# Attention, soft mixture of experts and a feed-forward layer in one kernel: the AV products of a pair of heads in one run, on nineteen exp tiles

## The chip, the cores and the metric

The kernel runs on one core of a Trainium2 chip. Its time is the device time of one execution in microseconds (us). The kernel before took 464.92 us, the median of three runs (464.62 to 466.56). One further execution was profiled.

## What is computed

Sixteen heads (2 batches of 8) of 768 tokens with 64 features. Each query and key is hashed by the signs of six projections, and a query attends only to keys of its own bucket. The output of attention is the input of a soft mixture of experts, and that of a feed-forward layer with g = h - tanh(h).

```python
q_bits = (np.einsum('bhsd,dk->bhsk', q, proj) > 0).astype(np.int64)
k_bits = (np.einsum('bhsd,dk->bhsk', k, proj) > 0).astype(np.int64)
mask = q_bucket[:, :, :, None] == k_bucket[:, :, None, :]
scores = np.where(mask, scale * np.matmul(q, k.transpose(0, 1, 3, 2)), -1000000000.0)
attn = np.exp(scores - np.max(scores, axis=-1, keepdims=True))
attn = attn / (np.sum(attn, axis=-1, keepdims=True) + 1e-09)
out = np.matmul(attn, v)
...
d = softmax of x @ phi over the tokens; slot_out[e] = np.maximum(slot_input[e] @ w1[e], 0.0) @ w2[e]
g = h - np.tanh(h)      # h = x @ w_in
return (g @ w_out).astype(np.float32)
```

## The kernel before, in words

Heads are worked on in eight pairs, 0 to 7. For each pair:

- xq and xk arrive by DMA. ScalarE (and GpSimd for pair 0) writes their high parts into the operands QA and KA (`his`, L378). The low parts go into QB and KB: by way of a PSUM tile `hp` that ScalarE writes (`hi_ps`, L407) and VectorE subtracts (`lo_ps`, L416), or on GpSimd for pair 0.
- The hash bits are four products with `projb` on 32 columns of the array (`pb`, L333; L355 for pairs 0 and 1), a comparison on VectorE, and rows of plus or minus a large number, placed below the features in QA and KA.
- The row maxima: 18 PSUM tiles `pm` (L444), each reduced by VectorE (L446). `m_fin` turns them with one product `pc` (L454), makes a row on VectorE (`zrow`, `row`, L457 and L458) and sends it by DMA into QA.
- The scores: 18 PSUM tiles `pst` (nine for each head; two products each, with QA and KA and then QB and KB, L503), each followed by an exponential on ScalarE into a tile `e` (L505) of the pool `e_p`, which has 12 tiles. GpSimd adds the tiles `e` up (L515).
- The AV products: nine units `a`. Each takes a tile of head 0 and one of head 1 against v (`tv`), both heads at once on 64 columns of the array (L532), into two PSUM tiles `pav`. A first product of `pav`, with `zrw` and `vzw` on all 128 columns (L526), opens each.
- Then come sums over `e` (`pr`, L546, on 32 columns), transposes (`prt`, `px`), and logits (`pl`).

Beside this, VectorE and ScalarE convert w_in from 64-bit numbers, in 16 pieces. One conversion is a ScalarE pass (`cg`, L179) and three VectorE passes (`cl`, `cl`, `win`, L183, L192, L197).

PSUM tiles of this stage come from six banks in turn. Every engine works through its instructions in the order in which the program issues them. That order is written out by hand: START is a list of units for the first stage, STEP a list for each of pairs 0 to 6, LAST that for pair 7. In them `m` is a tile of maxima, `s0` and `s1` one of scores of head 0 and 1, `a` an AV unit, `wl` and `wc` the loading and conversion of a piece of w_in, `g0` to `g2` and `l0` to `l2` the high and low parts, `lp` the loading of a piece of weights. A unit of which everything is done is skipped.

The weights of the experts arrive in pieces of 1 MB, in slots that are opened in groups (RING) as memory of the attention stage is given up. After attention comes the mixture of experts (from about 250 us), and from about 315 us the feed-forward loop.

Of the kernel before, what the change touches and what calls it, by code (L numbers as in the profile page):

```python
# [132 lines left out]
def body(ctx: ExitStack, tc: tile.TileContext, q, k, v, proj, phi, w1, w2, w_in, w_out, cst, out, dbg=None):  # L133
# [114 lines left out]
    def attention():  # L248
# [80 lines left out]
        def bits(i):  # L329
            pb = psum("pb")  # L330
            for g in range(4):
                x = (xqs, xks)[g // 2][i]
                nc.tensor.matmul(pb[32 * g:32 * g + 32, :HALF], projb, x[:, (g % 2) * HALF:(g % 2 + 1) * HALF],  # L333
                                 start=True, stop=True, tile_position=(0, 32 * g))
# [14 lines left out]
        def bits0(i, which):  # L349
            x = (xqs, xks)[which][i]  # L350
            w = (512, S - 512)
            bt0[which] = [e_p.tile([P, 512], F32, tag="e", name="bt0")[64:64 + 4 * NB, :n] for n in w]
            pbs = [psum("pb") for _ in w]
            for j, (c0, c1) in enumerate(((0, 512), (512, S))):
                nc.tensor.matmul(pbs[j][64:96, :w[j]], projb, x[:, c0:c1], start=True, stop=True, tile_position=(0, 64))  # L355
            for j in range(2):
                nc.vector.tensor_scalar(bt0[which][j], pbs[j][64:64 + 4 * NB, :w[j]], 0.0, None, ALU.is_gt)

        def rows0(i, which, h, eng):
            rs = slice(64, 64 + 4 * NB)  # L360
            X, o = ((QA, C_FIRST), (KA, C_FIRST + 2 + 2 * h))[which]
            w = ct[rs, o:o + 2]
            for (c0, c1), b, e in zip(((0, 512), (512, S)), bt0[which], "av" if eng == "s" else 2 * eng):
                y = X[i][h][rs, c0:c1]
                if e == "a":
# [328 lines left out]
        def unit(w, i):  # L694
            if w in ("m", "s0", "s1", "a", "ap", "wl", "wc", "lp", "warm", "keep", "const", "e"):
                if w == "m" and nm.get(i) == 2 * len(SEQ) - 1:
                    return
            elif (w, i) in done:
                return
            else:  # L700
                done.update({(w, i), (w.replace("hv", "h").replace("hp", "h").replace("lv", "l"), i)})
# [12 lines left out]
            elif w[:2] in ("bq", "bk"):  # L714
                bits0(i, "qk".index(w[1]))
            elif w[:2] in ("wq", "wk"):
                rows0(i, "qk".index(w[1]), int(w[2]), w[3])
# [682 lines left out]
```

## Time and profile before

| | |
|---|---|
| median of three runs | 464.92 us |
| the profiled execution | 464.5 us, its span 462.7 us |
| TensorE (PE) | 442.7 us busy, 96% of the span |
| VectorE (DVE) | 330.5 us, 71% |
| ScalarE (ACT) | 271.8 us, 59% |
| GpSimd (POOL) | 289.3 us, 63% |
| mean granted clock of TensorE | 0.99 |

A share of the whole span is a mean over three stages with different limits. Through the attention stage VectorE is busy for nine tenths and more, behind it less. TensorE counts as busy whenever one of its overlapping matmuls is under way, so that its share says little. What a matmul costs is the distance from its start to the start of the next one. Idle time stands in brackets with what ended it.

### The profile page before, as it was taken

The page shows a single profiled execution, that of the slowest core. Times are in us where ns is not written, and L with a number is a line of the kernel's source. Part 1 is how long each engine was busy: PE and PEld are TensorE (multiplying, and loading weights), DVE is VectorE, ACT ScalarE, POOL GpSimd, SP SyncE. Part 2 cuts the span into 40 slices and gives each one's busy share as a digit, 9 for nine tenths or more (in the row PEclk, how much of TensorE's full clock was granted, in tenths as well). Part 3 has the DMA queues.
Part 4 walks back from the last instruction along what each step waited for, and adds up shares of the span by engine and source line. Part 5 has one row for each costly group of instructions (what it writes and reads, how often), then busy time and mean ns, then how long its engine had stood idle before and what let it go on. Part 6 is the DMA issues. An engine that isn't in the chain of part 4 may idle for free. (4 is left out here: it accounts for less than half of the span.)

```text
span 462.7 us, 7587 instructions
## 1 busy us (share of the span) xinstructions
PE 442.7 (96%) x2639; PEld 296.6 (64%) x2639; DVE 330.5 (71%) x592; ACT 271.8 (59%) x521; POOL 289.3 (63%) x291
## 2 busy tenths in 40 slices
PE   7589999999999999999999999999999999999995
PEld 3455565656666575766765544567777778888883
DVE  3999798897989969577173438579998976544441
ACT  4526676756776565654450111278889887666661
POOL 4976977889697896958871110025888884444450
PEclk9889999999999999999999999999999999999998
DMA  6337337153633509449539999992000003000004
GB/s 195 110 98 221 125 98 219 41 170 127 189 125 106 167 15 298 178 142 326 216 157 379 421 416 417 419 419 83 2 1 2 0 0 137 1 1 1 0 1 144
DMA packets 18342, 71.32 MB, mean 154 GB/s; under 512 B 3668, under 2 KB 4792, under 8 KB 13176
## 3 DMA queue, kind: packets, MB, share of 16 engines
q1 hardware_dynamic: 17976, 70.75, 43.5%
q8 instruction: 23, 0.38, 0.4%
q14 instruction: 23, 0.19, 0.1%
q10 hardware_dynamic: 320, 0.01, 0.0%
HBM read 60.08 MB, written 3.15 MB: 137 GB/s over the span
## 5 line engine op out<-in xcount | busy, mean ns | idle before, releaser
L505 ACT ACTIVATE e<-pst 128x512 f32<-128x512 f32 x144 | 79.9, 598 | 44.6 <-PE pst L503 40.9
L515 POOL TENSOR_TENSOR es<-es,e 128x512 f32<-128x512 f32 x73 | 92.9, 1288 | 13.1 <-ACT e L505 13.0
L446 DVE TENSOR_REDUCE mx<-pm 128x1 f32<-128x512 f32 x144 | 90.2, 682 | 10.7 <-PE pm L444 9.8
L532 PE MATMUL pav<-e,tv 128*64 128x512 f32 (+1 forms) x384 | 70.5, 496 | 0.0
L503 PE MATMUL pst<-QA,KA 128*128 128x256 f32 (+1 forms) x192 | 67.7, 367 | 0.8 <-DVE mx L446 0.4
L503 PE MATMUL pst<-QB,KB 128*128 128x256 f32 (+1 forms) x192 | 62.2, 338 | 0.0
L1221 DVE SCALAR_TENSOR_TENSOR ph<-win,ph 128x512 f32<-128x512 f32 (+1 forms) x64 | 35.7, 558 | 32.2 <-ACT win L1216 30.8
L444 PE MATMUL pm<-KA,QA 96*128 96x512 f32 x192 | 51.5, 369 | 2.8 <-DVE QA L368 2.4
L1252 POOL TENSOR_TENSOR split<-win,split 128x512 fp32r<-128x512 f32 x31 | 44.8, 1447 | 14.2 <-ACT split L1247 14.2
L1273 PE MATMUL po<-w,split 128*128 128x512 f32 x128 | 51.0, 399 | 0.0
L1271 PE MATMUL po<-w,split 128*128 128x512 f32 x128 | 50.6, 396 | 0.0
L515 POOL TENSOR_TENSOR es<-e 128x512 f32<-128x512 f32 x30 | 39.2, 1316 | 18.1 <-PE pr L546 18.0
L1272 PE MATMUL po<-w,split 128*128 128x512 f32 x128 | 50.5, 394 | 0.0
L444 PEld LDWEIGHTS pm<-KA,QA 96*128 96x128 f32 x192 | 34.0, 197 | 24.1 <-ACT e L505 7.3
L503 PEld LDWEIGHTS pst<-QA,KA 128*128 128x128 f32 x192 | 36.1, 188 | 20.2 <-DVE mx L446 7.1
L1252 POOL TENSOR_TENSOR ghl<-win,ghl 128x256 fp32r<-128x256 f32 x32 | 24.2, 757 | 37.0 <-ACT ghl L1247 37.0
L1216 ACT ACTIVATE win<-ph 128x512 f32<-128x512 f32 (+1 forms) x64 | 30.8, 481 | 23.0 <-PE ph L1209 22.3
L1222 DVE SCALAR_TENSOR_TENSOR win<-win,ph 128x512 f32<-128x512 f32 (+1 forms) x64 | 35.5, 555 | 8.7 <-DVE ph L1221 0.5
L532 PEld LDWEIGHTS pav<-e,tv 128*64 128x64 f32 x384 | 24.1, 136 | 27.1 <-issue 20.4
L1217 ACT ACTIVATE win<-win,ct 128x512 f32<-128x512 f32 (+1 forms) x64 | 39.5, 617 | 2.1
L503 PEld LDWEIGHTS pst<-QB,KB 128*128 128x128 f32 x192 | 36.4, 189 | 2.0
L1273 PEld LDWEIGHTS po<-w,split 128*128 128x128 f32 x128 | 24.0, 188 | 7.7 <-POOL split L1252 2.7
(236 smaller groups left out, 818.4 us busy)
## 6 DMA issues: line engine op xcount, KB each, us to landing
w<-in_moe_w_dram SPq DMA_DIRECT2D x32, 1024.0 KB
raw<-in_moe_w_in_dram SPq DMA_DIRECT2D x16, 512.0 KB
w<-in_moe_w_out_dram SPq DMA_DIRECT2D x8, 1024.0 KB
xq<-in_q_dram SPq DMA_DIRECT2D x8, 384.0 KB
xk<-in_k_dram SPq DMA_DIRECT2D x8, 384.0 KB
tv<-in_v_dram SPq DMA_DIRECT2D x8, 384.0 KB
out_dram<-win SPq DMA_DIRECT2D x12, 256.0 KB
QB<-QA SPq DMA_DIRECT2D x10, 192.0 KB
```

The costliest lines, as they stand in the source:

```text
L444: nc.tensor.matmul(pm[:, j * 256:j * 256 + c1 - c0], QA[s][h][:96, c * P:(c + 1) * P], KA[s][h][:96, c0:c1], start=True, stop=True)
L446: nc.vector.reduce_max(m, pm.rearrange("p (c k) -> p c k", c=len(cs)), axis=AX.X)
L503: nc.tensor.matmul(pst[:, j * 256:j * 256 + c1 - c0], K[h][:, c * P:(c + 1) * P], Q[h][:, c0:c1], start=x == 0, stop=x == 1)
L505: nc.scalar.activation(e, pst, AF.Exp, scale=0.125)
L515: eng.tensor_tensor(q[0], y, e, ALU.add)
L532: nc.tensor.matmul(pav[i][k][64 * h:64 * h + 64, :], tv[i][:, h, c, :], e2[h][:, j * 256:j * 256 + c1 - c0], start=False, stop=c == KT - 1 ...
L1217: nc.scalar.activation(w, z, AF.Square, bias=ct[:, C_QA:C_QA + 1])
L1221: nc.vector.scalar_tensor_tensor(self.ph[p], z, Q_C, self.ph[p], ALU.mult, ALU.mult)
L1252: (eng or nc.gpsimd).tensor_tensor(gl[p], g, gh[p].bitcast(F32), ALU.subtract)
L1271: nc.tensor.matmul(po, gh[p][:, us], wo.half(f, 0), start=f == 0, stop=False)
L1272: nc.tensor.matmul(po, gh[p][:, us], wo.half(f, 1), start=False, stop=False)
L1273: nc.tensor.matmul(po, gl[p][:, us], wo.half(f, 0), start=False, stop=f == NF - 1)
```

## The change

- Nineteen tiles `e` in place of twelve for pairs 0 to 5: seven come from a new pool `ex_p`, which is given up in pair 6. Eighteen tiles hold all the exponentials of a pair.
- New lists of units. FIRST is for pair 0, STEP for pairs 1 to 5, STEP2 for pair 6; START is rewritten, LAST is as it was. In STEP the nine AV units of the pair before stand at the head, then the scores and the maxima.
- `fy` and `vy` are `fz` and `v2` (the rows for `zrw`, `vzw`) of the same pair in place of the next.
- For pairs 0 and 1 the bits are one PSUM tile of four products on 32 columns, compared in place (VectorE reads and writes PSUM), and the rows are written from there. Before it was two tiles for each of q and k, compared into four tiles of `e_p`.
- `projb` arrives laid out by the host, in one DMA in place of a memset and four.
- One slot for weights less is opened after pair 5 and one more in pair 6.

```diff
+WIDE, NE1, NE2 = 5, 12, 7
-RING, HOLD = (4, 2, 2, 4, 3, 2, 3, 1), 4
+RING, HOLD = (4, 1, 3, 4, 3, 2, 3, 1), 4
-STEP = ("a a a m xe s0 g1 m a m l1 s1 s0 s1 m s0 m m g0 l0 m xr s1 h1 m m s0 m a m m wl m g2 s1 lp l2 s0 v wl a d m wc "
+STEP = ("a a a a a a a a wc a d g0 l0 fy h1 g1 wc l1 g2 h0 h3 lp l2 vy m m wl s0 m lp s0 s1 v xe m m qk m s0 m e xr b m "
...
     def consts2(phiB, projb, blk):
-        nc.vector.memset(projb, 0.0)
-        for h in range(2):
-            for j in range(2):
-                c0 = 2 * NB * h + NB * j
-                nc.scalar.dma_start(out=projb[64 * h:64 * h + 64, c0:c0 + NB], in_=proj)
+        nc.scalar.dma_start(out=projb, in_=proj)
...
-        e_p = pool("e_p", 12)
+        e_p = pool("e_p", NE1)
...
+        ex_p = pool("ex_p", NE2, wide_x)
...
-        def bits0(i, which):
-            x = (xqs, xks)[which][i]
-            w = (512, S - 512)
-            bt0[which] = [e_p.tile([P, 512], F32, tag="e", name="bt0")[64:64 + 4 * NB, :n] for n in w]
-            pbs = [psum("pb") for _ in w]
-            for j, (c0, c1) in enumerate(((0, 512), (512, S))):
-                nc.tensor.matmul(pbs[j][64:96, :w[j]], projb, x[:, c0:c1], start=True, stop=True, tile_position=(0, 64))
+        def halves(i, pb):
+            for g in range(4):
+                x = (xqs, xks)[g // 2][i]
+                nc.tensor.matmul(pb[32 * g:32 * g + 32, :HALF], projb, x[:, (g % 2) * HALF:(g % 2 + 1) * HALF],
+                                 start=True, stop=True, tile_position=(0, 32 * g))
+
+        def bits0(i):
+            pb = bt0[i] = psum("pb")
+            halves(i, pb)
+            nc.vector.tensor_scalar(pb[:, :HALF], pb[:, :HALF], 0.0, None, ALU.is_gt)
+
+        def rows0(i, which, h, eng):
+            X, o = ((QA, C_FIRST), (KA, C_FIRST + 2 + 2 * h))[which]
             for j in range(2):
...
+                rs = slice(32 * (2 * which + j), 32 * (2 * which + j) + 4 * NB)
+                y, b, w = X[i][h][64:64 + 4 * NB, j * HALF:(j + 1) * HALF], bt0[i][rs, :HALF], ct[rs, o:o + 2]
...
-            e = e_p.tile([P, 512], F32, tag="e", name="e")
+            turn[0] += i <= WIDE
+            e = (ex_p if i <= WIDE and turn[0] % (NE1 + NE2) >= NE1 else e_p).tile([P, 512], F32, tag="e", name="e")
...
-            for u in STEP if i < NPR - 1 else LAST:
+            for u in FIRST if i == 0 else STEP if i <= WIDE else STEP2 if i < last else LAST:
...
-                if i == 6 and len(slots) == sum(RING[:2]) and not xqs and not xks:
+                if i == 6 and len(slots) == sum(RING[:2]) and not xqs and not xks and (not queue or queue[0][0] > WIDE):
                     xq_x.close()
+                    wide_x.close()
                     open_ring(RING[2], rctx)
```

The tables move instructions. The first place is TensorE around the AV products of a pair in the middle of the stage. `pav` are the AV products, and `pst` and `pm` scores and maxima. Before, one of a pair's visits to the 64 columns follows the other after eight matmuls on 128:

```order
L526 MATMUL pav<-zrw,vzw 128x512
L532 MATMUL pav<-e,tv 64x512 x2
L444 MATMUL pm<-KA_135,QA_131 128x512
L444 MATMUL pm<-KA_135,QA_131 128x256 x2
L444 MATMUL pm<-KA_135,QA_131 128x512
L503 MATMUL pst<-QA_130,KA_134 128x512
L503 MATMUL pst<-QB_138,KB_141 128x512
L503 MATMUL pst<-QA_129,KA_133 128x512
L503 MATMUL pst<-QB_137,KB_140 128x512
L532 MATMUL pav<-e,tv 64x512 x2
L444 MATMUL pm<-KA_135,QA_131 128x512
```

In the changed kernel, the same products of one pair:

```order
L457 MATMUL pc<-ct,mh 12x128
L532 MATMUL pav<-zrw,vzw 128x512
L538 MATMUL pav<-e,tv 64x512 x4
L532 MATMUL pav<-zrw,vzw 128x256
L538 MATMUL pav<-e,tv 64x256 x4
L538 MATMUL pav<-e,tv 64x512 x4
L538 MATMUL pav<-e,tv 64x256 x4
L538 MATMUL pav<-e,tv 64x512 x4
L538 MATMUL pav<-e,tv 64x256 x4
L490 MATMUL pv<-va,ones_62 128x128
L447 MATMUL pm<-KA_135,QA_131 128x512 x2
```

All nine units stand between `pc` and the next pair's maxima, with only the second `zrw` product among them. Before, a pair's AV products stand in five such runs (2, 2, 6, 2 and 12 matmuls).

The second place is TensorE at the bits (`pb`) and the sums (`pr`), both on 32 columns. Before, the bits follow the fourth AV run and stand apart from the sums:

```order
L532 MATMUL pav<-e,tv 64x512 x2
L454 MATMUL pc<-ct,mh 12x128
L333 MATMUL pb<-xq,projb 32x384 x2
L333 MATMUL pb<-xk,projb 32x384 x2
L503 MATMUL pst<-QA_129,KA_133 128x256
L503 MATMUL pst<-QB_137,KB_140 128x256
L503 MATMUL pst<-QA_129,KA_133 128x256
L503 MATMUL pst<-QB_137,KB_140 128x256
```

In the changed kernel:

```order
L447 MATMUL pm<-KA_135,QA_131 128x512
L552 MATMUL pr<-es_706,ones_62 32x384
L552 MATMUL pr<-es_807,ones_62 32x384
L552 MATMUL pr<-es_706,ones_62 32x128
L552 MATMUL pr<-es_807,ones_62 32x128
L552 MATMUL pr<-es_873,ones_62 32x256
L552 MATMUL pr<-es_909,ones_62 32x256
L355 MATMUL pb<-xq,projb 32x384 x2
L355 MATMUL pb<-xk,projb 32x384 x2
L447 MATMUL pm<-KA_135,QA_131 128x512
```

The bits now stand right behind the sums. With the AV products, a pair now goes three times to fewer than 128 columns, where it went seven times.

The third place is VectorE at the end of a pair's maxima. Before, the conversion of a piece of w_in comes behind the bits and the reciprocals, while maxima and low parts are spread over the pair:

```order
L451 TENSOR_REDUCE mh<-mx 128x12
L457 TENSOR_SCALAR zrow<-pc 12x128
L458 SCALAR_TENSOR_TENSOR row<-zrow,pc 12x128
L336 TENSOR_SCALAR bt<-pb 128x384
L570 TENSOR_SCALAR rs<-prt 128x6x2
L573 RECIPROCAL rs<-rs 128x12
L183 TENSOR_SCALAR cl<-raw 128x512
L192 SCALAR_TENSOR_TENSOR cl<-cg,cl 128x512
L197 SCALAR_TENSOR_TENSOR win<-raw,cl 128x512
```

In the changed kernel:

```order
L449 TENSOR_REDUCE mx<-pm 128x2
L454 TENSOR_REDUCE mh<-mx 128x12
L460 TENSOR_SCALAR zrow<-pc 12x128
L461 SCALAR_TENSOR_TENSOR row<-zrow,pc 12x128
L188 TENSOR_SCALAR cl<-raw 128x512
L197 SCALAR_TENSOR_TENSOR cl<-cg,cl 128x512
L202 SCALAR_TENSOR_TENSOR win<-raw,cl 128x512
L419 TENSOR_TENSOR KB_143<-xk,hp 64x512
L419 TENSOR_TENSOR KB_144<-xk,hp 64x512
L188 TENSOR_SCALAR cl<-raw 128x512
L197 SCALAR_TENSOR_TENSOR cl<-cg,cl 128x512
L202 SCALAR_TENSOR_TENSOR win<-raw,cl 128x512
```

Two conversions and the eight low parts (`KB`, `QB`; two are seen here) now stand together behind `mh` and `pc`, which is to say beside TensorE's AV run.

The fourth place is VectorE at the program's start. Before:

```order
L301 MEMSET QA_128 64x1536
L357 TENSOR_SCALAR bt_168<-pb 24x512
L357 TENSOR_SCALAR bt_169<-pb 24x256
L357 TENSOR_SCALAR bt_176<-pb 24x512
L357 TENSOR_SCALAR bt_177<-pb 24x256
L368 TENSOR_SCALAR QA_128<-bt_176,ct 24x512
L368 TENSOR_SCALAR QA_128<-bt_177,ct 24x256
L446 TENSOR_REDUCE mx<-pm 128x1 x2
```

In the changed kernel:

```order
L307 MEMSET QA_131 64x1536
L174 MEMSET ones_62 128x32
L361 TENSOR_SCALAR pb<-pb 128x384
L371 TENSOR_SCALAR QA_131<-pb,ct 24x384 x2
L449 TENSOR_REDUCE mx<-pm 128x1 x2
L449 TENSOR_REDUCE mx<-pm 128x2
L449 TENSOR_REDUCE mx<-pm 128x1 x2
```

One comparison in PSUM stands for four, and the rows of QA come in equal halves.

## Rows read from the trace of the kernel before

**Rows 1.** The page's first line, the profiled span
```profile
span 462.7 us, 7587 instructions
```

**Rows 2.** Stretches: length, busy us (count) of engines, clock, DMA share, GB/s
```profile
94.60:122.10 27.50, 27.50 (x167) 17.16 (x166) 24.73 (x46) 18.53 (x35) 22.93 (x24) 1.00 0.45 135
242.00:290.00 48.00, 46.98 (x424) 24.10 (x424) 24.06 (x45) 5.96 (x12) 4.85 (x17) 1.00 0.98 401
```

**Rows 3.** Waits of PE, 60 to 245 us: total, times, longest
```profile
PE pm L444 <- DVE cl L192: 0.2, 1, 0.2
```

**Rows 4.** PE in order of time: start us, length us, line, tiles, count
```profile
111.25 3.66 PE L532 MATMUL pav<-e,tv 128*64 128x256 f32 x24
...
138.82 3.66 PE L532 MATMUL pav<-e,tv 128*64 128x256 f32 x24
142.41 0.50 PE L444 MATMUL pm<-KA,QA 96*128 96x512 f32 x1
...
142.99 0.40 PE L503 MATMUL pst<-QB,KB 128*128 128x512 f32 x1
143.22 0.63 PE L444 MATMUL pm<-KA,QA 96*128 96x512 f32 x3
143.69 0.40 PE L503 MATMUL pst<-QA,KA 128*128 128x512 f32 x1
...
152.48 0.40 PE L503 MATMUL pst<-QB,KB 128*128 128x512 f32 x1
152.80 1.08 PE L532 MATMUL pav<-e,tv 128*64 128x512 f32 x4
153.81 0.73 PE L444 MATMUL pm<-KA,QA 96*128 96x512 f32 x3
154.38 0.28 PE L503 MATMUL pst<-QA,KA 128*128 128x256 f32 x1
```

**Rows 5.** Waits of DVE over two pairs: first and last of six
```profile
DVE mx L446 <- PE pm L444: 1.1, 2, 0.6
...
DVE bt L336 <- PE pb L333: 0.4, 2, 0.2
```

**Rows 6.** DVE in order of time, one pair from 94.6 us
```profile
94.47 4.28 DVE L446 TENSOR_REDUCE mx<-pm 128x1 f32<-128x512 f32 x7
98.78 0.85 DVE L416 TENSOR_TENSOR KB<-xk,hp 64x256 fp32r<-64x256 f32 x2
...
101.24 0.69 DVE L183 TENSOR_SCALAR cl<-raw 128x512 uint32<-128x512 uint32 x1
...
103.38 2.47 DVE L446 TENSOR_REDUCE mx<-pm 128x2 f32<-128x512 f32 x4
...
106.69 0.28 DVE L457 TENSOR_SCALAR zrow<-pc 12x128 fp32r<-12x128 f32 x1 [0.56 <-PE pc L454]
...
117.29 1.37 DVE L416 TENSOR_TENSOR QB<-xq,hp 64x512 fp32r<-64x512 f32 x2
```

**Rows 7.** ACT in order of time, one conversion
```profile
109.18 0.67 ACT L179 ACTIVATE cg<-raw 128x512 f32<-128x512 f32 x1
```

**Rows 8.** The first stage in order of time, all engines
```profile
1.20 2.48 ACTq L167 DMA_DIRECT2D projb<-in_proj_dram  x4
...
1.58 0.43 SPq L320 DMA_DIRECT2D xk<-in_k_dram  x1
...
5.37 0.84 ACT L378 ACTIVATE KA<-xk 64x768 fp32r<-64x768 f32 x1 [0.37 <-DMA xk<-in_k_dram]
...
11.27 2.36 DVE L368 TENSOR_SCALAR QA<-bt,ct 24x512 fp32r<-24x512 f32 x2
...
13.96 5.47 DVE L446 TENSOR_REDUCE mx<-pm 128x1 f32<-128x512 f32 x9 [0.33 <-PE pm L444]
...
54.42 0.56 DVE L336 TENSOR_SCALAR bt<-pb 128x384 f32<-128x384 f32 x1 [0.22 <-PE pb L333]
...
60.27 1.36 DVE L446 TENSOR_REDUCE mx<-pm 128x1 f32<-128x512 f32 x2
```

More of the change, by code (lines that the diff above doesn't have):

```diff
@@ L61 @@
 FORD = [4 * q + 2 * h + i for h in range(2) for q in range(4) for i in range(2)]
-RING, HOLD = (4, 2, 2, 4, 3, 2, 3, 1), 4
-START = ("warm.4 const.1 qk.0 const.0 hp2.0 keep.1 oi.0 const.2 h0.0 bk.0 bq.0 keep.3 wq0v.0 kc.0 wl.0 keep.3 wk0a.0 "
[3 rows of a table removed]
-        "keep.1 oi.2 wl.0").split()
-STEP = ("a a a m xe s0 g1 m a m l1 s1 s0 s1 m s0 m m g0 l0 m xr s1 h1 m m s0 m a m m wl m g2 s1 lp l2 s0 v wl a d m wc "
-        "lp v1 e m s0 s0 a wl a lp a e s1 lp m m h0 s1 s0 qk m v2 h3 s1 e lp a f2 lp b s0 x2 e fz wc s1 wc s1 lg lp h2 "
-        "x3 a a wl lp").split()
+RING, HOLD = (4, 1, 3, 4, 3, 2, 3, 1), 4
+START = ("oi.0 qk.0 h1.0 const.1 const.0 warm.4 const.2 keep.1 hp3.0 keep.3 h0.0 wl.0 b0.0 wk0a.0 hp2.0 kc.0 wq0v.0 wl.0 "
+        "m.0 keep.1 m.0 m.0 qk.1 l1.0 m.0 wk1a.0 m.0 m.0 m.0 m.0 keep.1 m.0 v.0 wq1a.0 m.0 keep.3 m.0 m.0 keep.3 m.0 "
+        "v1.0 d.0 h2.1 h3.1 l0.0 m.0 fa.0 m.0 m.0 m.0 h1.1 v.1 oi.1 keep.1 b0.1 m.0 l3.0 fb.0 h0.1 wc.0 wq0a.1 wl.0 "
+        "kc.1 s0.0 keep.1 l2.0 oi.2 wl.0 qk.2 fz.0 wk1a.1 s0.0 wk0v.1 s0.0 wc.0 a.0 wq1a.1 s0.0 v2.0 wc.0 s0.0 s0.0").split()
+FIRST = ("wc wc lp lp a a a a a a a g0 g1 h1 fy wl m vy g2 l0 a a l1 l2 s0 h0 s0 s1 m m s1 s1 v m wl m h3 qk m m d m m "
+        "xe s1 h2 b m m s0 m e wl lg m s1 m s1 m s0 lp e s0 wl xr v1 lp m x3 x2 m s1 s0 s1 e m s1 lp lp s0 s0 f2 s0 s0 "
+        "wc s1 e").split()
+STEP = ("a a a a a a a a wc a d g0 l0 fy h1 g1 wc l1 g2 h0 h3 lp l2 vy m m wl s0 m lp s0 s1 v xe m m qk m s0 m e xr b m "
+        "h2 x2 m m v1 wl s0 lp m s1 lp s0 m m lg x3 s1 m m s1 m s0 m wc e s0 s0 s1 s1 s1 m wl s0 s1 s0 lp lp e s1 f2 e "
+        "s1 wl").split()
+STEP2 = ("m m a a a a a a vy s0 a a a a fy g1 l1 m s0 s0 m a m s1 h1 m s0 s1 m m m s1 g0 wl m xe d l0 xr m m v s0 v1 a a "
+        "e s1 g2 m l2 a a m lp m e e lp lp s0 wl s1 wl lp b x2 qk wc s1 m m s0 v2 e lp m s1 wc h2 a a a f2 wc h3 lp h0 "
+        "fz lp s0 wl s0 s1 x3 s1 lg lp").split()
 LAST = ("a a s0 a lp xe a a a s0 lp lp a a lp s0 s0 lp s0 s1 s1 s0 s1 xr s0 s1 s1 lp s1 s1 lp a a lp a s0 x2 s1 s0 lg "
@@ L120, in constants @@
                     o = C_FIRST + 2 * (g // 2 + g // 2 * h)
-                    c[2 * D // 2 + 2 * NB * h + j, o:o + 2] = m, a
+                    for j2 in range(2):
+                        c[row + 32 * j2, o:o + 2] = m, a
     k = np.float32(np.float32(EPS) / np.float32(S))
@@ L257, in attention @@
         es_p = pool("es_p", 1)
-        e_p = pool("e_p", 12)
+        e_p = pool("e_p", NE1)
         tv_p = pool("tv_p", 1)
-        last_x, head_x, early_x, xq_x, mid_x, raw_x = (ExitStack() for _ in range(6))
+        last_x, head_x, early_x, wide_x, xq_x, mid_x, raw_x = (ExitStack() for _ in range(7))
         opsL = [None, pool("opsL1", 1, last_x)]
@@ L330, in bits @@
             pb = psum("pb")
[L331 to L334, printed above, removed]
+            halves(i, pb)
             bt = pre.tile([P, HALF], F32, tag="bt", name="bt")
@@ L347, in attention @@
         bt0 = {}
-        def bits0(i, which):
-            x = (xqs, xks)[which][i]
-            w = (512, S - 512)
-            bt0[which] = [e_p.tile([P, 512], F32, tag="e", name="bt0")[64:64 + 4 * NB, :n] for n in w]
-            pbs = [psum("pb") for _ in w]
-            for j, (c0, c1) in enumerate(((0, 512), (512, S))):
-                nc.tensor.matmul(pbs[j][64:96, :w[j]], projb, x[:, c0:c1], start=True, stop=True, tile_position=(0, 64))
-            for j in range(2):
[L357 to L365, printed above, removed]
+        def halves(i, pb):
[5 more added lines that the diff above has]
+            pb = bt0[i] = psum("pb")
+            halves(i, pb)
+            nc.vector.tensor_scalar(pb[:, :HALF], pb[:, :HALF], 0.0, None, ALU.is_gt)
+        def rows0(i, which, h, eng):
+            X, o = ((QA, C_FIRST), (KA, C_FIRST + 2 + 2 * h))[which]
+            for j in range(2):
+                rs = slice(32 * (2 * which + j), 32 * (2 * which + j) + 4 * NB)
+                y, b, w = X[i][h][64:64 + 4 * NB, j * HALF:(j + 1) * HALF], bt0[i][rs, :HALF], ct[rs, o:o + 2]
+                if eng[j % len(eng)] == "a":
                     nc.scalar.activation(y, b, AF.Identity, bias=w[:, 1:2], scale=w[:, 0:1])
                 else:
-                    {"v": nc.vector, "p": nc.gpsimd}[e].tensor_scalar(y, b, w[:, 0:1], w[:, 1:2], ALU.mult, ALU.add)
+                    nc.vector.tensor_scalar(y, b, w[:, 0:1], w[:, 1:2], ALU.mult, ALU.add)
         def his(i, n, eng=None):
@@ L495, in v_unit2 @@
             vz[i] = vzw
+        turn = [-1]
         def s_unit(i, h, n):
@@ L713, in unit @@
                     nc.tensor.matmul(wt[0][:32, :w_], wz[:, :32] if w == "warm" else ident[:, :32], wz if w == "warm" else ident, start=True, stop=True)
[L714 to L715 removed]
+            elif w == "b0":
+                bits0(i)
             elif w[:2] in ("wq", "wk"):
[L717 removed]
+                rows0(i, "qk".index(w[1]), int(w[2]), w[3:])
             elif w == "lp":
@@ L1367, in laid_out @@
         return a.reshape(B, H // 2, 2, P, KT, D).transpose(0, 1, 3, 2, 4, 5).reshape(B, H // 2, P, S)
+    if name == "proj":
+        p = np.zeros((P, 32), a.dtype)
+        for h in range(2):
+            for j in range(2):
+                p[64 * h:64 * h + 64, 2 * NB * h + NB * j:2 * NB * h + NB * (j + 1)] = a
+        return p
     if name == "moe_w1":
```

3 lines of the change are left out of this document (2 added, 1 removed), and 3 rows, old and new, of the table START.

## Prediction

> **What bounds the kernel now.** I read the stretches first, then TensorE's waits, then TensorE's starts in order of time, then VectorE's waits and its instructions, and last the program's start. In the middle of attention, from 94.6 to 122.1 us, TensorE is busy for the whole 27.5 us at full clock, VectorE for 24.7, GpSimd for 22.9 and ScalarE for 18.5 [rows 2]. From 60 to 245 us TensorE has 0.2 us of waits in all [rows 3]. So in that stage the time is the sum of TensorE's starts, and one pair takes 27.57 us (from the long AV run at 111.25 to that at 138.82 [rows 4]). Whatever shortens TensorE's list there shortens the kernel, until VectorE, the next one, is full.
>
> **What one visit to 64 columns costs TensorE.** Take u as the time of one group of 512 columns, both heads, and x as what a visit adds inside itself. The long run, 24 records or eight such groups by columns, lasts from 138.82 to 142.41, 3.59 us; the short run, two groups, from 152.80 to 153.81, 1.01 us. So 6u = 2.58, u = 0.43 and x = 0.15. Outside it, the score product ahead of the visit takes 0.32 us to the next start (152.48 to 152.80) where 0.23 is usual (142.99 to 143.22), and the maxima behind it 0.57 (153.81 to 154.38) where the same three take 0.47 (143.22 to 143.69). That is 0.15 + 0.09 + 0.10 = 0.34 us a visit [rows 4].
>
> **The middle, pairs 1 to 4.** The order shows seven visits to fewer than 128 columns a pair before (five AV runs, bits, sums) and three in the changed kernel: AV, AV behind the second `zrw` product, and sums with bits in one. Four visits less are 4 x 0.34 = 1.36 us, so TensorE alone would need 27.57 - 1.36 = 26.2 us. That the sums and bits count as one is a choice: no row shows them side by side. The Trainium skill, page "TensorEngine Tiling (Array Packing)", section Tiling Modes, says that a change of the tiling mode, and not of the tile alone, drains the array; by it two neighbours on 32 columns are one visit and 64 and 32 columns are two modes. If they were two visits, TensorE would need 26.5.
>
> VectorE does the same work for a pair as before. Its six kinds of waits over two pairs (1.1 at the top, 0.4 at the bottom [rows 5]) are 4.3 us together, so it is occupied for 27.57 - 2.15 = 25.4 us a pair. One wait stays: between `mh` and `zrow` it waits 0.56 us for TensorE's `pc` [rows 6]; in the new order nothing stands between them. That makes 26.0. What is new is when its work is to be had. During an AV run, 12 x 0.43 x 1.5 = 7.7 us and with `zrw` and the visits' costs 8.7, (twelve groups of 512 columns and twelve of 256) TensorE makes no maxima. VectorE has under it: the wait and two short rows (1.2), two conversions of 2.14 (101.24 to 103.38), eight low parts (2 x 1.37 of 512 and 2 x 0.85 of 256, 4.4 us), 9.9 us in all [rows 6]. So the run is covered, and VectorE comes out of it about 1 us late; the tail of the pair, where TensorE makes scores for 4 us and VectorE has one conversion and one maximum (2.8), gives it back. One thing can be late: the first conversion under the run needs ScalarE's `cg` (0.67 [rows 7]), which stands behind the last exponentials. I add that 0.6: VectorE then sets the pace at 26.6 us a pair, and four pairs gain 4 x (27.57 - 26.6) = 3.9 us. The bounds of a pair are 26.2 (TensorE alone) and, upward, a run with nothing under it: 26.0 + 8.7 is the far end, which I do not believe since the work stands in the list; to 28.9 it is a rival below.
>
> The seven more tiles `e` cost no instruction. They let all 18 exponentials of a pair wait for the run; nineteen is one to spare, so the next pair's second exponential waits for the first AV unit. ScalarE has 9 us a pair free for that [rows 2]. GpSimd's sums are the same; it is at 22.9 of 27.5 and would be at 86% of 26.6.
>
> **Pairs 5 to 7.** Visits go from 14 to 10 up to the end of pair 6, again 4 x 0.34 = 1.4 us; pair 7 has the same list. The conversions are over by then, so I let TensorE keep the pace.
>
> **The start.** VectorE bounds it. xk is read 3.8 us after its issue (1.58 to 5.37). xq now goes out first, two issues of 0.43 ahead of xk's 1.58, at 0.7, so it is there at 4.5; ScalarE copies it (0.84) and only then issues `projb`, at 5.4. When `projb` lands no row shows: at the earliest at once, at the latest 3.8 us on as with xk; I take 2.2. Four products, one comparison (0.56), two row halves, products and the first maximum follow: some 3.4 us, at 11.0 (between 8.8 and 12.6) in place of 13.96 [rows 8]. The row halves are the doubtful part: today's two take 2.36 us at 11.27 for 24 rows [rows 8]. I take 1.0, by the pass over 128 rows in 0.56. The Trainium skill, page "SBUF — State Buffer" (its notes on the port pair that VectorE and GpSimd share), says that a VectorE pass in a two-port mode and a GpSimd pass lock each other out; a source in PSUM would not take that lock. By the rule it is 1.0, without it 2.4.
>
> From the first maximum to the first of pair 2 VectorE then has 36 maxima at 0.61 (4.28 for seven [rows 6]), 22.0; two turns through `pc`, 2.5, and a third under the run, 1.4; five conversions, 10.7; sixteen low parts, 8.8; two comparisons, 1.1; four short passes, 1.5; and 0.8 of waiting for `cg`. That is 48.8, to 59.8, where it stands at 60.27 now [rows 8]. So of 3 us won at the start 0.5 are left: the low parts of pair 2, 4.4 us, are now done before its maxima and not among them. Earlier scores of pair 0 gain nothing, since VectorE has its list to do anyway. Bounds: 2.5 lost to 3.4 won.
>
> **What costs nothing.** Each weight piece moved is 1 MB, 2.6 us at the 401 GB/s of the later stretch [rows 2]. Eight pieces are issued before pair 7 as before, and the saturated stretch begins when pair 7's slots open, which moves with attention. If that cover went, one piece's 2.6 us would show.
>
> **Sum.** 3.9 + 1.4 + 0.5 = 5.8 us. The profiled execution took 464.5 (span 462.7 [rows 1]); it becomes 458.7, and the median of 464.92 becomes 459.1.
>
> **Rivals.**
> *TensorE keeps the pace.* VectorE finds its work in time, 26.2 a pair: 5.4 + 1.4 + 3.0 at the start = 9.8, 455.1 us. For it speaks that VectorE's 26.0 is below 26.2; against it that the two are 0.2 apart and wait for each other.
> *The waits eat the gain.* Six PSUM banks hold `cl`, `hp`, `pm` and `pst` in turn; behind the run TensorE's third and fourth tile need banks that VectorE's low parts still hold. At 1 us of this a pair takes 27.5, and only 1.4 + 0.5 is left: 463.0.
> *The run starves VectorE.* If `cg` and `hp` come so late that VectorE idles 2.9 us a pair on top of its 26.0, a pair takes 28.9: 4 x 1.33 lost, less 1.9, is 3.4 us slower, 468.3. It decides from an idle time of 2.0 us a pair (1.57 + 1.9/4). For it: all of VectorE's work under the run hangs on ScalarE, which comes to it behind eight exponentials that TensorE makes in 4 us. Against it: ScalarE's part of that work, two `cg`, four `hp`, is 3.5 us of 8.7.
>
> **How the numbers follow.** My forecast has 0.48, TensorE's pace 0.22, the eaten gain 0.16, the starved run 0.14. A measurement of this kernel can tell about 0.5%, 2.3 us, from no change. Faster are TensorE's pace, 0.46 of the forecast (all but the start at its worst) and 0.04 of the eaten gain (a good start), 0.72; the same are the rest of these two and 0.01 of the starved run, 0.15; slower is what is left of the starved run, 0.13. The 8-in-10 range reaches to the first rival below and into the last above: 455.0 to 465.5. The likeliest case alone spans 457 to 461.5.
>
> **What would show it.** The profile after should have AV runs of some 8.7 us, 26.3 to 26.9 us apart for pairs 0 to 4; the visits' price of 0.34 unchanged; waits of TensorE for VectorE in the tens of a us a pair right behind the run; VectorE's first maximum near 11 and the first of pair 2 near 60 us; and everything behind attention the same, only shifted. I am wrong on the start if pair 2's first maximum stands outside 57 to 63, on the middle if the runs are over 27.3 apart, and on the mechanism if TensorE's starts around a run do not show 0.34 a visit.

## The result and the profile after

The changed kernel takes 460.25 us (median of four runs, 459.11 to 461.1) and the kernel before 465.28 beside it (464.62 to 466.56): a ratio of 0.9886, with a 95% interval of 0.9866 to 0.9905. It is faster, by 5.0 us between the medians. The profiled executions are 3.7 us apart: 464.5 us before, 460.77 after, whose span (the page's first line) answers to [rows 1]:

```profile
span 459.0 us, 7553 instructions
```

The stretches of the kernel after, in the columns of [rows 2]: the first 20 us of VectorE's maxima, one pair in the middle, and the stretch of the weights' stream.

```profile
10.00:20.00 10.00, 9.41 (x29) 5.95 (x30) 8.18 (x14) 6.00 (x9) 1.16 (x2) 0.51 0.95 249
20.00:30.00 10.00, 7.58 (x31) 3.80 (x30) 7.70 (x17) 2.98 (x6) 9.52 (x13) 0.67 0.15 43
88.98:115.12 26.14, 26.14 (x168) 17.85 (x167) 24.52 (x46) 18.21 (x34) 22.85 (x24) 1.00 0.52 145
237.60:285.60 48.00, 47.12 (x424) 24.08 (x424) 24.20 (x45) 5.96 (x12) 4.87 (x17) 1.00 0.98 402
```

The middle pair is 1.4 us shorter than before with TensorE still full for all of it; the weights' stream reads as it did. From 60 to 245 us TensorE's waits are this one, in pair 6 [rows 3]:

```profile
PE pst L508 <- ACT vhi L494: 0.7, 1, 0.7
```

TensorE in order of time behind pair 2's maxima, and at its sums and bits (before: [rows 4]):

```profile
105.40 0.27 PE L457 MATMUL pc<-ct,mh 128*12 128x128 f32 x1
105.56 0.47 PE L532 MATMUL pav<-zrw,vzw 128*128 128x512 f32 x1
105.96 1.94 PE L538 MATMUL pav<-e,tv 128*64 128x512 f32 x8
107.83 0.39 PE L532 MATMUL pav<-zrw,vzw 128*128 128x256 f32 x1
108.15 6.24 PE L538 MATMUL pav<-e,tv 128*64 128x256 f32 x40
114.32 0.49 PE L490 MATMUL pv<-va,ones 128*128 128x128 f32 x2
...
118.25 0.86 PE L552 MATMUL pr<-es,ones 128*32 128x384 f32 x12
118.92 0.49 PE L355 MATMUL pb<-xq,projb 128*32 128x384 f32 x1
```

The run lasts from 105.56 to 114.32, 8.8 us. VectorE under this run (before: [rows 6]), with no wait listed from `row` to the next pair's first maximum at 115.40:

```profile
105.00 0.18 DVE L454 TENSOR_REDUCE mh<-mx 128x12 f32<-128x24 f32 x1
105.71 0.28 DVE L460 TENSOR_SCALAR zrow<-pc 12x128 fp32r<-12x128 f32 x1 [0.53 <-PE pc L457]
...
106.23 0.68 DVE L188 TENSOR_SCALAR cl<-raw 128x512 uint32<-128x512 uint32 x1
...
114.31 0.85 DVE L419 TENSOR_TENSOR QB<-xq,hp 64x256 fp32r<-64x256 f32 x2
115.19 0.28 DVE L493 TENSOR_TENSOR vt<-pv,blk 4x128 f32<-4x128 f32 x1
115.40 4.27 DVE L449 TENSOR_REDUCE mx<-pm 128x1 f32<-128x512 f32 x7
```

Over pairs 1 to 3, from 62.96 to 141.20 us, the only wait of VectorE over half a microsecond in all is this; before there were others ([rows 5]), `cg` among them, which the second line shows for two pairs of the kernel before:

```profile
DVE zrow L460 <- PE pc L457: 1.6, 3, 0.6
...
DVE cl L192 <- ACT cg L179: 0.8, 2, 0.4
```

The first stage, all engines (before: [rows 8]):

```profile
3.72 0.37 ACTq L172 DMA_DIRECT2D projb<-in_proj_dram  x1
...
6.39 0.71 PE L355 MATMUL pb<-xq,projb 128*32 128x384 f32 x1
...
7.75 0.57 DVE L361 TENSOR_SCALAR pb<-pb 128x384 f32<-128x384 f32 x1 [4.77 <-PE pb L355]
...
8.40 1.34 ACT L369 ACTIVATE KA<-pb,ct 24x384 fp32r<-24x384 f32 x2 [2.85 <-DVE pb L361]
...
9.78 1.37 DVE L371 TENSOR_SCALAR QA<-pb,ct 24x384 fp32r<-24x384 f32 x2 [1.46 <-ACT KA L369]
...
10.59 0.76 PE L447 MATMUL pm<-KA,QA 96*128 96x512 f32 x1 [2.96 <-DVE QA L371]
...
11.39 0.69 DVE L449 TENSOR_REDUCE mx<-pm 128x1 f32<-128x512 f32 x1 [0.24 <-PE pm L447]
```

The bits come early, but TensorE then idles 2.96 us for the row halves, and from 10 to 20 us its granted clock is 0.51, the lower of its two levels (1.2 GHz of 2.4). The kernel before has 0.99 in that stretch and falls later:

```profile
10.00:20.00 10.00, 4.23 (x29) 3.00 (x25) 9.02 (x14) 7.30 (x11) 8.49 (x11) 0.99 0.47 174
20.00:30.00 10.00, 8.46 (x29) 5.20 (x28) 9.61 (x18) 0.00 (x0) 6.94 (x7) 0.67 0.43 118
...
19.77 0.37 PE L454 MATMUL pc<-ct,mh 128*6 128x128 f32 x1 [3.37 <-DVE mh L451]
```

In that later fall TensorE was ahead: its 3.37 us of idle ended at 19.77 with `mh` of VectorE, and VectorE waits only 0.3 us for `pm` from 8 to 63 us. What VectorE does in the kernel after, where it had nine maxima without a gap before:

```profile
12.68 5.47 DVE L449 TENSOR_REDUCE mx<-pm 128x1 f32<-128x512 f32 x9 [0.60 <-PE pm L447]
19.11 1.29 DVE L449 TENSOR_REDUCE mx<-pm 128x1 f32<-128x512 f32 x2 [0.95 <-PE pm L447]
21.23 1.29 DVE L449 TENSOR_REDUCE mx<-pm 128x1 f32<-128x512 f32 x2 [0.84 <-PE pm L447]
```

Where the 3.7 us of the two profiles are, by TensorE's first scores of each pair and the end of its last AV product:

| stretch | before | after | shorter by |
|---|---|---|---|
| start to first scores of pair 1 | 60.04 | 62.96 | -2.9 |
| from there to those of pair 5 (pairs 1 to 4) | 110.27 | 105.12 | 5.15 |
| from there to the last AV product | 79.00 | 76.83 | 2.2 |
| behind it | 213.4 | 214.1 | -0.7 |

The first scores of pairs 1 to 4 are 26.02, 26.14 and 26.08 us apart, where it was 27.59, 27.55 and 27.57; the fourth stretch, with three small products that stood in the next pair before, has 26.88 for 27.56. Of the 0.7 us behind attention some 0.4 fall behind TensorE's last product.

### The profile page after: what moved, and what is told of

Same layout as the page of the kernel before. It is cut to its first block, busy times and chain, and to the rows that moved or that the text cites. A ratio compares the mean times of both kernels' runs of the same rounds, so it can differ in the third digit from the quotient of the medians.

```text
span 459.0 us, 7553 instructions
## 1 busy us (share of the span) xinstructions
PE 437.5 (95%) x2621; PEld 300.1 (65%) x2621; DVE 325.5 (71%) x585; ACT 272.9 (59%) x525; POOL 286.5 (62%) x287
## 5 line engine op out<-in xcount | busy, mean ns | idle before, releaser
L511 ACT ACTIVATE e<-pst 128x512 f32<-128x512 f32 x144 | 78.5, 604 | 39.0 <-PE pst L508 36.1
L508 PE MATMUL pst<-QA,KA 128*128 128x256 f32 (+1 forms) x192 | 66.3, 359 | 3.9 <-ACT QA L369 1.3
L538 PE MATMUL pav<-e,tv 128*64 128x512 f32 (+1 forms) x384 | 66.6, 491 | 0.0
L447 PE MATMUL pm<-KA,QA 96*128 96x512 f32 x192 | 55.2, 381 | 3.8 <-DVE QA L371 3.0
L447 PEld LDWEIGHTS pm<-KA,QA 96*128 96x128 f32 x192 | 35.2, 207 | 18.5 <-issue 9.3
L538 PEld LDWEIGHTS pav<-e,tv 128*64 128x64 f32 x384 | 25.7, 136 | 31.4 <-issue 24.8
```

The source lines that it names most:

```text
L447: nc.tensor.matmul(pm[:, j * 256:j * 256 + c1 - c0], QA[s][h][:96, c * P:(c + 1) * P], KA[s][h][:96, c0:c1], start=True, stop=True)
L508: nc.tensor.matmul(pst[:, j * 256:j * 256 + c1 - c0], K[h][:, c * P:(c + 1) * P], Q[h][:, c0:c1], start=x == 0, stop=x == 1)
L511: nc.scalar.activation(e, pst, AF.Exp, scale=0.125)
L538: nc.tensor.matmul(pav[i][k][64 * h:64 * h + 64, :], tv[i][:, h, c, :], e2[h][:, j * 256:j * 256 + c1 - c0], start=False, stop=c == KT - 1 ...
```

## Experiments

Each ran on one chip together with others, next to the kernel before. "Pair spacing" is the distance between VectorE's first maxima of pairs 2, 3, 4 in the profiled execution: 26.1 us in the changed kernel, 27.56 before.

### What a visit to fewer columns costs

```diff
-STEP = ("a a a a a a a a wc a d g0 l0 fy h1 g1 wc l1 g2 h0 h3 lp l2 vy m m wl s0 m ..."
+STEP = ("a a a m a a a m a a wc a d g0 l0 fy h1 g1 wc l1 g2 h0 h3 lp l2 vy wl s0 m ..."
```

> The new kernel with the AV products of pairs 0 to 4 (those in the list of pairs 1 to 5) in three runs instead of one, one maximum unit between each two: two visits more in each of five pairs, no instruction more. Theory A (TensorE sets the pace and a visit costs it 0.34 us): 26.1 + 0.68 = 26.8 us from pair to pair, 5 x 0.68 = 3.4 us, 463.7 us. Rival D (VectorE sets the pace, as the forecast had it, or what the change won lies elsewhere than in the visits): pairs stay within 0.2 of 26.1, 460.3 to 461.3 us.

497.12 us, 1.0692 of before (1.0644 to 1.074), pair spacing 34.1 us: far outside both. The two maxima stand ahead of the conversions in VectorE's own order too, so VectorE waits for them inside the run:

```profile
126.06 0.69 DVE L449 TENSOR_REDUCE mx<-pm 128x1 f32<-128x512 f32 x1 [3.44 <-PE pm L447]
129.22 0.69 DVE L449 TENSOR_REDUCE mx<-pm 128x1 f32<-128x512 f32 x1 [2.47 <-PE pm L447]
```

That is 5.9 us of idle VectorE a pair; TensorE then waits for VectorE in its turn, and its granted clock falls to 0.90 on the mean of such a pair. Of the price of a visit this says nothing. It shows the starved run of the forecast's last rival, from the other side: what stands first in VectorE's list under the run decides.

The same cut with scores, which leave VectorE's list alone:

```diff
+STEP = ("wc d g0 l0 h1 g1 wc l1 g2 a a a fy s0 a a a s1 a a a h0 h3 lp l2 vy m m wl m lp s0 ..."
```

> The new kernel with the AV run of pairs 0 to 4 (in the list of pairs 1 to 5) cut into three by the first two score units that stood behind it; VectorE's list is the same to the instruction, ScalarE's has two exponentials before two copies. Two visits more in five pairs. Theory A (TensorE sets the pace, a visit costs 0.34 us): pairs 26.1 + 0.68 = 26.8 us apart, 460.3 + 3.4 = 463.7 us. Rival D (visits cost little by themselves, or VectorE sets the pace): within 0.3 us of 26.1, 460.3 to 461.5 us.

465.58 us, 1.0037 of before (1.0007 to 1.0067); attention ends 4.6 us later than in the changed kernel. The pair spacing is 27.1 us, with TensorE full:

```profile
109.54 1.08 PE L538 MATMUL pav<-e,tv 128*64 128x256 f32 x8
110.56 0.50 PE L508 MATMUL pst<-QA,KA 128*128 128x512 f32 x1
111.22 2.80 PE L538 MATMUL pav<-e,tv 128*64 128x512 f32 x16
113.95 0.50 PE L508 MATMUL pst<-QA,KA 128*128 128x512 f32 x1
114.61 2.80 PE L538 MATMUL pav<-e,tv 128*64 128x512 f32 x16
117.34 0.49 PE L490 MATMUL pv<-va,ones 128*128 128x128 f32 x2
```

A pair takes 1.0 us more. TensorE's starts tell how much of it the two visits cost: from 109.54 to 117.34 these 40 AV records and four score products take 7.80 us. In the changed kernel 40 such records take 6.17 (108.15 to 114.32), and four score products are 0.94 at the usual 0.23 to 0.24. The rest, 0.69 us, is 0.34 a visit. The other 0.3 us a pair falls 9 us ahead of the run, at three maxima that the cut doesn't touch: 0.77 us to the next start where the changed kernel has 0.48. The first two lines are of this version, the last two of the changed kernel:

```profile
97.45 0.93 PE L447 MATMUL pm<-KA,QA 96*128 96x256 f32 x3
98.22 1.45 PE L617 MATMUL pl<-phiB,xtu 128*128 128x64 f32 x12
...
96.34 0.64 PE L447 MATMUL pm<-KA,QA 96*128 96x256 f32 x3
96.82 1.45 PE L617 MATMUL pl<-phiB,xtu 128*128 128x64 f32 x12
```

The profile lists no wait there. That TensorE, with two score tiles fewer ahead of these maxima, waits for PSUM tiles which VectorE still has to read would fit, and is not shown. Cutting the run into three gives back all that the change won in time, some two thirds of it by the visits themselves. So visits do cost TensorE what the forecast said.

```diff
-STEP = ("... m e xr b m h2 x2 ..."
+STEP = ("... m e xr m b h2 x2 ..."
```

> The new kernel with one maximum unit put between the sums and the bits in the list of pairs 1 to 5, in place of behind both. If sums and bits beside each other count as one visit, as the forecast chose: one visit more a pair, 26.1 + 0.34 to 0.50 = 26.4 to 26.6 us from pair to pair, 1.7 to 2.5 us in all, 462 to 463 us. If they are two visits already: 26.1 as now, 460.3 us.

461.43 us, 0.9937 of before (0.9911 to 0.9963), where the changed kernel on the same chip has 0.9897. The pair spacing is 26.4: one maximum between sums and bits makes a second visit of 0.29 us (the mean over the first scores of pairs 1 to 4). Side by side the two are one visit.

### Who sets the pace in the middle

```diff
+                    for _ in range(1 + (w == h == 0 and 2 <= i <= WIDE)):
-                    nc.vector.tensor_tensor(o[:, c0:c1], (xks, xqs)[x][i][hs, c0:c1], ...)
+                        nc.vector.tensor_tensor(o[:, c0:c1], (xks, xqs)[x][i][hs, c0:c1], ...)
```

> The new kernel with one low part of 512 columns done twice for pairs 2 to 5, under the AV run: 0.69 us more for VectorE in four pairs, nothing else. By the forecast (VectorE sets the pace of pairs 1 to 4 and waits only for what it lists): 4 x 0.69 = 2.8 us more, 463.1 us. By the trace as I read it now (TensorE sets the pace, VectorE has 0.7 to 0.8 us of waits a pair): under 0.3 us a pair, 460.3 to 461.3 us.

462.4 us, 0.9966 of before (0.9937 to 0.9996). The pair spacing is 26.5, 0.4 more for 0.69 of VectorE's work: between the two expectations. Compared start by start with the changed kernel, TensorE loses it in four steps of 0.04 to 0.24 us, 0.7 to 2.2 us behind a pair's first scores. That would fit tiles that wait for PSUM banks which VectorE, late by then, has not read; the profile lists no wait there. So TensorE sets the pace of the changed kernel, but only just: VectorE has some 0.3 us a pair to spare.

### Start and middle apart

```diff
-START = ("oi.0 qk.0 h1.0 const.1 ... b0.0 wk0a.0 ...")      # and the bits in place
+START = ("warm.4 const.1 qk.0 ... bk.0 bq.0 ... a.0 qk.2 s0.0 s0.0 wc.0 s0.0 s0.0 wc.0 wk1a.1 s0.0 s0.0 keep.1 oi.2 wl.0")   # and the bits of before
```

> The old start (its bits, its START list with the six first score units put into its end) with the new lists from pair 0 on and the wide ring of e tiles. Theory A (the new start is what loses: TensorE at the half clock and VectorE waiting for it): the first scores of pair 1 come at 60.0 us as before instead of 62.96, the pairs stay 26.1 apart, so 460.3 - 2.9 = 457.4 us. Rival B (the loss belongs to pair 0's new list, whose long AV run and low parts of pair 2 stand ahead of pair 1's scores): the first scores of pair 1 at about 63 again, 460.3 us.

465.21 us, 1.0027 of before (0.9992 to 1.0061): neither. The profiled execution took 470.21, 5.0 us above the median. In it this mixture brought two waits of 3.6 us each of VectorE in the start, for `cg` and for a piece of w_in (`DVE cl <- DMA raw`), which neither kernel has; the first scores of pair 1 come at 69.9. How much of that the median has is not shown, so the run tells nothing about the start. But the first scores of pairs 1 to 4 are 26.0, 26.7 and 26.1 us apart: the middle's gain doesn't hang on the new start.

```diff
-            for u in FIRST if i == 0 else STEP if i <= WIDE else STEP2 if i < last else LAST:
+            for u in STEP_BEFORE if i < last else LAST:
```

> The new start with the old list of a pair for pairs 0 to 6. Theory A (the start loses): the pairs 27.57 apart again and the first scores of pair 1 some 2.9 us later than before, 465.3 + 2.9 = 468.2 us. Rival B (the new start is worth its earlier first maximum, 11.4 against 14.0, and only pair 0's new list loses it): 465.3 - 2.5 = 462.8 us. Halfway, 465.3, if VectorE has its list to do anyway and the half clock hides under it.

466.79 us, 1.0046 of before (1.0013 to 1.008). In the profiled execution (470.0, above the median) the first scores of pair 1 come at 63.62, pair 1 takes 29.43 us, and from pair 2 on the pairs are 27.57 apart again. The new start loses time with the old lists too, as theory A had it, though 2.1 us by the ratio where it said 2.9.

### What the start loses by

`keep.n` are filler products of TensorE on a tile that nothing reads.

```diff
-START = ("... b0.0 wk0a.0 ... m.0 m.0 m.0 m.0 keep.1 m.0 v.0 ... m.0 fa.0 m.0 m.0 m.0 h1.1 ..."
+START = ("... b0.0 keep.11 wk0a.0 ... keep.2 m.0 m.0 m.0 keep.2 m.0 keep.1 m.0 v.0 ... m.0 keep.5 fa.0 keep.2 m.0 m.0 m.0 keep.3 h1.1 ..."
```

> The new kernel with more filler products on TensorE in the start only: eleven behind the bits, where TensorE idles 3.0 us, and some between the maxima of pair 0. Theory A (half clock from 10.6 us makes VectorE wait 2.4 us for its maxima): granted clock 1.0 from 10 to 20 us, VectorE's waits there under 0.5, pair 1's first scores near 60.5, 457.9 us. Rival C (VectorE has its list to do anyway, or waits for ScalarE's row halves): the clock goes up, but pair 1's first scores stay within 0.5 us of 62.96, 460.3 us.

458.57 us, 0.9865 of before (0.983 to 0.9901). The clock is held, and the waits for `pm` go:

```profile
10.00:20.00 10.00, 9.70 (x56) 6.29 (x57) 9.48 (x17) 5.24 (x8) 0.79 (x1) 1.00 0.90 240
```

But pair 1's first scores come only 1.0 us earlier, which is less than the 2.1 us between two profiles of the changed kernel (the table below). What stood behind the clock is a wait of ScalarE for GpSimd's zero fills of pair 1's operands, and VectorE's 2.31 us behind that:

```profile
26.31 1.34 ACT L370 ACTIVATE QA<-pb,ct 24x384 fp32r<-24x384 f32 x2 [5.18 <-POOL QA L308]
```

In the changed kernel GpSimd has been idle ahead of those fills, since the sums of V stand before them in its list:

```profile
POOL va L482 <- DMA tv<-in_v_dram: 11.3, 1, 11.3
```

```diff
-START = ("... v1.0 d.0 h2.1 h3.1 l0.0 m.0 fa.0 ... h1.1 v.1 oi.1 keep.1 b0.1 ..."
+START = ("... l0.0 d.0 h2.1 h3.1 m.0 fa.0 ... h1.1 v.1 oi.1 v1.0 keep.1 b0.1 ..."
```

> The new kernel with one step of GpSimd moved in the start: the sums of pair 0's V, for which GpSimd waits 11.3 us (7.4 to 18.8), go behind the zero fills of pair 1's operands and pair 0's third low part. Nothing else changes. Theory G (what holds the start back is GpSimd's list, full from 18.8 to 46 us because it idled before): the fills and the low part are done by about 14 us, GpSimd's first sum of exponentials starts some 5 us before 35.9, pair 1's first scores come 1 to 2 us before 62.96, 458.3 to 459.3 us. Rival A (the half clock alone, and VectorE waiting for it): the half clock from 10.6 us stays, so does pair 1's first score at 62.96 within 0.5, 460.3 us.

459.92 us, 0.9898 of before (0.9867 to 0.9928): no gain by itself. GpSimd is early and now waits 9.5 us for exponentials; the half clock stays (0.63 from 10 to 20 us, 0.50 from 20 to 30).

> The fillers of the run before that held the clock, and GpSimd's step moved, together. Theory A with G (with the clock held, the next wait is ScalarE's row halves of pair 1, that wait for GpSimd's zero fills until 26.3 us): VectorE's wait of 2.3 us for these row halves goes, pair 1's first scores come 2 to 3 us before 62.96, 457.3 to 458 us. Rival (the two don't add up: scores wait for the exponentials' or another list): as the fillers alone, 458.6 to 459 us and pair 1's first scores at 62.

457.85 us, 0.9871 of before (0.9841 to 0.9901). VectorE's wait for the row halves is gone, and pair 1's first scores come at 59.58, 3.4 us before those of the changed kernel, and 5.5 before those of its second profile. The table sets the start's kernels side by side, in us of their profiled executions; the third column is what VectorE's 36 maxima of pairs 0 and 1 take up, each counted from its start to the start of VectorE's next instruction.

| kernel | first maximum | 36 maxima | first maximum to that of pair 2 | first scores of pair 1 |
|---|---|---|---|---|
| before | 13.96 | 22.0 | 46.3 | 60.04 |
| changed | 11.39 | 24.9 | 51.8 | 62.96 |
| changed, once more | 12.63 | 25.7 | 52.7 | 65.09 |
| fillers | 10.62 | 22.5 | 51.5 | 61.96 |
| GpSimd's step moved | 12.21 | 25.5 | 52.5 | 64.50 |
| both | 10.50 | 22.5 | 49.3 | 59.58 |
| both, bits in SBUF | 11.01 | 22.4 | 50.0 | 60.71 |
| both, more fillers | 12.44 | 22.6 | 49.4 | 61.59 |

```diff
-            nc.vector.tensor_scalar(pb[:, :HALF], pb[:, :HALF], 0.0, None, ALU.is_gt)
+            bt0[i] = e_p.tile([P, 512], F32, tag="e", name="bt0")
+            nc.vector.tensor_scalar(bt0[i][:, :HALF], pb[:, :HALF], 0.0, None, ALU.is_gt)
```

> As the run with fillers and GpSimd's step moved, and the start's bits compared into a tile in SBUF instead of in place in PSUM. Theory S (row halves of ScalarE and VectorE take turns because both read one PSUM tile: VectorE waits 1.46 us for ScalarE's): the two run beside each other, the first maximum comes at 9.2 instead of 10.6, another 0.5 to 1.4 us off the start. Rival (the order of the two is set by something else, such as the target tiles): the wait of 1.46 stays and the time is that of the run without this edit.

458.4 us, 0.9885 of before (0.9855 to 0.9915): no gain. The turns do end, VectorE's halves start right behind the comparison. But from SBUF they take 2.00 and 1.00 us in place of 0.67 each, and each ends 0.2 us behind the GpSimd pass beside it (a low part and a fill):

```profile
7.94 2.00 DVE L373 TENSOR_SCALAR QA<-bt,ct 24x384 fp32r<-24x384 f32 x1
9.97 1.00 DVE L373 TENSOR_SCALAR QA<-bt,ct 24x384 fp32r<-24x384 f32 x1
...
7.92 1.80 POOL L431 TENSOR_TENSOR KB<-xk,KA 64x768 fp32r<-64x768 f32 x1
10.03 0.74 POOL L304 MEMSET zrw<- 128x768 f32 x1
```

From PSUM, in the changed kernel, two halves of pair 1 take 1.38 us together beside such a low part:

```profile
30.73 1.38 DVE L371 TENSOR_SCALAR KA<-pb,ct 24x384 fp32r<-24x384 f32 x2 [0.27 <-ACT KA L369]
...
29.94 1.84 POOL L433 TENSOR_TENSOR KB<-xk,kh 64x768 fp32r<-64x768 f32 x1
```

The last two stood on one chip: the changed kernel again, and the version with both edits and twelve fillers more among the start's last scores.

```diff
-START = ("... s0.0 wk0v.1 s0.0 wc.0 a.0 wq1a.1 s0.0 v2.0 wc.0 s0.0 s0.0")
+START = ("... s0.0 wk0v.1 s0.0 keep.2 wc.0 a.0 wq1a.1 s0.0 v2.0 keep.5 wc.0 s0.0 s0.0 keep.5")
```

> The changed kernel once more, to stand on one chip beside the version with fillers and GpSimd's step moved: 460.3 us, 0.989 of before.

> The run with fillers and GpSimd's step moved, and twelve fillers more among the last scores of the start, where TensorE idled 3 us from 28.9 to 33 and its clock was at a half until 38.4. If the clock there still matters: pair 1's first scores at 58.5 to 59 instead of 59.58, 457 us and 2 to 3 us below the changed kernel beside it. If VectorE and ScalarE set that stretch alone: 59.6 again, 457.9 us.

The changed kernel has 460.26 us (458.97 to 463.02) and 0.9897 of before (0.987 to 0.9925); the version with more fillers 457.76 (456.11 to 458.83) and 0.9844 (0.9813 to 0.9874). All its six runs lie below all six of the changed kernel: it beats both kernels, the changed one by 2.5 us. Its clock is 1.00 from 30 to 40 us too, where the version with both edits has 0.66, but from the first maximum on it takes as long as that one (49.4 and 49.3): there the clock no longer matters. Against the version with both edits the times leave it undecided.

## Why the prediction was right in its time, and where its steps failed

The forecast was 459.1 us, within 457 to 461.5 for its likeliest case, and the time is 460.25. Its sum of 5.8 us against 3.7 (profiled) and 5.0 (medians) hides errors of opposite sign: the middle and pairs 5 to 7 gave 2.0 us more than forecast, the start 3.4 less. That the total came out so near is in part luck.

**The visits: right.** Seven a pair became three, the four gone are worth 1.4 to 1.6 us in pairs 1 to 3 (forecast 1.36), sums and bits beside each other count as one, and cut runs give the gain back. Measured prices lie about the 0.34 of the forecast: 0.29 for the bits set apart, 0.34 for the cuts in the AV run, 0.37 on the mean of the four removed.

**The pace of the middle: the term of 0.6 us for `cg` failed.** The forecast had VectorE at 26.6 and TensorE alone at 26.2. Measured are 26.0 to 26.1, below the 26.3 to 26.9 that it named, and the waits of TensorE for VectorE that it expected behind the run are not listed. VectorE doesn't wait for `cg` in pairs 1 to 3: in the run shown, ScalarE's `cg` lasts from 106.17 to 106.89, and VectorE's pass on it starts at 107.01. So the first rival, TensorE keeping the pace, is what happens there: pairs 1 to 4 give 5.15 in place of 3.9 (that rival's 455.1 counted 3.0 us for the start as well, which were not won). That the two are close was read rightly.

**Pairs 5 to 7: 2.2 in place of 1.4**, in the right direction. With pair 4, whose stretch took over three small products, these stretches have 17 visits in place of 25 (neighbours on fewer than 128 columns counted as one; 7 became 4 in pair 4, and the forecast's 14 to 10 is 14 to 9), and the eight fewer are worth 2.9 us, after TensorE's new wait of 0.7 in pair 6.

**The start: wrong, and outside its bounds.** Pair 2's first maximum stands at 63.17, outside the 57 to 63 that the forecast named as its own test; first scores lose 2.9 us where 0.5 were to be won, and the bound was 2.5. The first maximum is as forecast (11.39 for 11.0), by two errors: `projb` came sooner (issued at 3.72 for 5.4, the products start at 6.39), and the row halves took 1.37 for 1.0 and 1.46 of waiting for ScalarE before that. The step that failed is "36 maxima at 0.61, 22.0": they took 24.9. It let VectorE's own list set the time, as in the kernel before, and took it for granted that TensorE would have its tiles there. With TensorE at the lower clock it had not. Where the clock is held and GpSimd's list is put in order, VectorE's list takes 49.3 us (forecast 48.8), and pair 2's first maximum stands at 59.81, the forecast's 59.8 (half a us sooner to the first maximum, half a us longer from there). With the clock held alone VectorE's list still takes 51.5 us (51.8 and 52.7 in the changed kernel), since ScalarE's rows waited for GpSimd, a second wait that the forecast did not have; with GpSimd's step moved alone it takes 52.5. Both hindrances were real, each hidden by the other.

How large the start's loss is in an undisturbed mean stays open. The first maximum came between 10.4 and 12.8 us in seven profiled executions with the same list ahead of it, and the two profiles of the changed kernel differ by 2.1 us at pair 1's first scores.

**On the row halves' price** the forecast leaned on a rule. The halves take 0.67 us each from PSUM, and 2.00 and 1.00 from SBUF beside GpSimd's passes; what was mis-sized is the pass itself (1.37 for two in place of 1.0). The Trainium skill, "SBUF — State Buffer", section "SBUF: two separate sides", says that the pair of ports which VectorE's two-port passes share with GpSimd is locked by whichever starts first, for the whole instruction. The trace agrees: GpSimd's low part starts at 7.92 and ends at 9.72, and VectorE's first half, started at 7.94, ends at 9.94; from PSUM nothing of the kind shows.

**What cost nothing** did cost nothing: the stretch of the weights' stream has 402 GB/s and the same busy times.

## What to carry to other kernels

When a table of order is rewritten, price the engine that waits as well as the one that works: a wait of 3 us of TensorE, cheap by itself, put it at the lower clock for the next 10 us and made it late for the engine that bounded the stage. Read each engine's own list for the first step that waits on a DMA, since all that stands behind it waits too; mending one such wait may show nothing until the next is mended. Products on fewer columns belong in one run, but only if the engine that lives on TensorE's other products has its other work ahead of them in its own list.

## What the runs showed of the hardware

- A visit to products on 64 or 32 columns and back costs TensorE 0.29 to 0.37 us among products on 128 columns at full clock; products on 32 columns of two kinds beside each other share one switch.
- After 2.96 us of idle TensorE had a granted clock of 0.51 from 10 to 20 us though it was busy for 9.4 of these 10; with fillers in that gap and between the maxima it was 1.00.
- VectorE and ScalarE, reading different rows of one PSUM tile, took turns in this program: 1.46 and 1.44 us of waiting at 9.78 and 11.18 us. With the tile in SBUF neither waited for the other. The Trainium skill, "PSUM — Partial Sum Buffer", section "PSUM bank collisions raise a hardware error", asks for turns only within one bank and the same 32 rows; the halves here lie on different ones, and no run here tried them at once.
- A VectorE pass that reads and writes SBUF (24 rows of 384 f32) ended 0.20 to 0.22 us behind the GpSimd pass that ran beside it, four times of four with the bits in SBUF (9.94 behind 9.72, 10.97 behind 10.77, 28.38 behind 28.16, 29.84 behind 29.63). The same pass from PSUM took 0.67 to 0.69 us.
